# Scores and weights of two of four batch pairs: each half of 64 queries gets a key band of its own

## The chip, the cores and the metric

The kernel runs on one core of one Trainium2 chip. The metric is the device time of one execution in microseconds; the time before is the median of three timed runs. All counts below are of one execution.

## The reference

Eight heads of causal attention with a window of 128 keys and a distance bias, then a two-layer MLP on the concatenated heads. What matters of it:

```python
window, scale = 128, 1.0 / np.sqrt(D)                    # B, H, S, D = 8, 8, 576, 64
scores = scale * np.matmul(q, k.transpose(0, 1, 3, 2))
rel = pos[:, None] - pos[None, :]
mask = (rel >= 0) & (rel < window)
scores = np.where(mask, scores + slopes * (-abs(rel)), -1e9)
attn = np.exp(scores - scores.max(-1))
x = (attn / (attn.sum(-1) + 1e-9)) @ v                   # -> 4608 tokens x 512
h = x @ w_in                                             # 512 x 2048
out = (h * sigmoid(h)) @ w_out                           # 2048 x 512
```

A query at position t attends to positions t-127 to t. A block of 128 queries therefore needs 255 keys, and a half block of 64 queries needs 191.

## The kernel before

**Blocks and pairs.** Two of the eight batches are laid end to end, so there are four batch pairs ("batches" 0 to 3 in the code) of 1152 rows, each of nine blocks of 128 rows: 36 blocks `i`, of which `i >= 18` belong to batches 2 and 3. A block is worked off in two pairs `p = 2i + q`; a pair is four heads, `u` in 0, 1 and `h` in 0, 1. Pairs 36 to 71 are those of batches 2 and 3. Block 0 of a batch pair has no block ahead of it; blocks 4 and 5 (`SPLIT`, `SPLIT + 1`) hold the seam between the two batches.

**One pair, step by step.** `scores` (L510) multiplies the 128 queries by the two key blocks `i - 1` and `i` into two PSUM tiles `sp`, one for each `h`. From batch 2 on, queries and keys are float16 in two parts, so each product is three matmuls (L517 to L523): 24 a pair, 12 in block 0. `h` 0 lies in rows 0 to 63 of the array and `h` 1 in rows 64 to 127, so two matmuls of 64 rows and 128 columns of weights stand side by side. `other_batch` (L533) writes the mask over keys of the other batch, `row_max` (L542) adds the bias table `tab` and takes the row maximum on VectorE, `exps` (L557) runs the exponential on ScalarE. `p_hi` (L572, ScalarE) and `p_lo` (L578; GpSimd for `u` 0, VectorE for `u` 1) split the weights into two float16 parts in a tile `hr` of 128 x 1024, one for each `u`. `p_transpose` (L588) issues one DMA transpose from SyncE's queue for each `u`, into `hl`. `attend` (L613) multiplies by the values: 24 matmuls of 128 x 128 weights and 64 or 65 columns, 12 in block 0. `normalize`, `x_hi`, `x_lo` and `x_dma` pass the result on to the MLP.

**The MLP around it.** Nine groups `g` of 512 tokens go through `gemm1` (L926; the matmuls are L949, L954 or, in the last two groups, L892 and L921) and `gemm2` (L1149; L1165, later L1068). Their matmuls are the bulk of TensorE's work, and a pair's `scores` and `attend` stand between them.

**What sets the order.** All instructions are recorded in the order of a hand-written plan: the loop steps through `pos`, and at each point first runs what `put(point, fn, ...)` has laid there, then one half of `gemm1` or `gemm2` (12 matmuls of 512 columns for most groups). Pair `p` has its scores at point `n = at(p)` (7 or 8 points after those of the pair ahead), `row_max` at n+1, `p_hi` at n+3 and n+4, `p_lo` and `p_transpose` at n+5, `attend` at n+11 or n+12. Each engine takes its instructions strictly in that order.

**Buffers.** `hr` has two buffers, `hl` four, one for each `u`. The tag `w1_2` is a weight tile that is done with before point 150. The scores' PSUM tiles and those of `attend` share the two banks of tag `a`.

Of the kernel before, what the change touches and what calls it, by code (L numbers as in the profile page):

```python
# [6 lines left out]
F32 = mybir.dt.float32  # L7
# [76 lines left out]
X_SUMS = {(NG - 2, 1): X7, (NG - 1, 0): X8, (NG - 1, 1): X9}  # L84
NB = 2
# [61 lines left out]
def tile_window_attention_then_silu_mlp(ctx, tc, qk, v, w_in, w_out, distance, out):  # L147
# [212 lines left out]
    def rescale_bias(b):  # L360

        ratio = vsc[b][:, 8:9] if b > QK16 else vsc[b][:, 7:8]
        flat = tab.rearrange("p h c -> p (h c)")
        nc.vector.tensor_scalar_mul(flat, flat, ratio)
# [140 lines left out]

    def blocks(p):

        return slice(1 if block_of(p // 2) == 0 else 0, 2)

    def scores(p):  # L510
        i, q = divmod(p, 2)
        tags = ("w", "x") if p == 2 * GT else next_tag("scores")
        sp = [ps_of(tags[h], f"sp{p}_{h}").rearrange("p (u o c) -> p u o c", u=2, o=2) for h in range(2)]
        for u in range(2):
            for o in range(blocks(p).start, 2):
                if i >= QK16 * NBLK:
                    for n, (a, b) in enumerate(((0, 0), (1, 0), (0, 1))):  # L517
                        for h in range(2):
                            rows = slice(h * D, (h + 1) * D)
                            nc.tensor.matmul(  # L520
                                sp[h][:, u, o], q16[i][rows, a, 2 * q + u], k16[i - 1 + o][rows, b, 2 * q + u],
                                start=n == 0, stop=n == 2, skip_group_check=True,
                            )  # L523
                    continue
# [17 lines left out]
    def row_max(p, k):  # L542
# [3 lines left out]
        scale, least, op = (1.0, -3.0e38, ALU.max) if b >= QK16 else (-0.125, 3.0e38, ALU.min)  # L546
        for u, h in [(k, 0), (k, 1)] if p < 2 * GT else [(0, k), (1, k)]:
# [9 lines left out]
    def exps(p, u):  # L557
# [6 lines left out]
        for h in range(2):  # L564
            x = t[:, h, 2 * P - n :]
            nc.scalar.activation(x, x, AF.Exp, bias=mx[:, 2 * u + h : 2 * u + h + 1], scale=scale)  # L566

    def split_of(p, u, what):
        n = 2 - blocks(p).start
        return what[:, : 4 * n * P].rearrange("p (a h c) -> p a h c", a=2, h=2)  # L570

    def p_hi(p, u):  # L572
        t, n = st[p]["t"][u], (2 - blocks(p).start) * P
        st[p]["hr", u] = hr = pool.tile([P, 8 * P], F16, tag="hr", bufs=2, name=f"hr{p}_{u}")
# [3 lines left out]
    def p_lo(p, u):  # L578
        t, n = st[p]["t"][u], (2 - blocks(p).start) * P
        hr = split_of(p, u, st[p]["hr", u])  # L580
        if p >= LOW_POOL:
            minus(nc.vector if LOW_DVE and u == LOW_U else nc.gpsimd, hr[:, 1], t[:, :, 2 * P - n :], hr[:, 0])
            return
# [20 lines left out]
    def p_copy_first(p, u):  # L604
        n = 2 - blocks(p).start
        st[p]["hl"][u] = hl = pool.tile([P, 4, P], F32, tag="hl", bufs=4, name=f"hl{p}_{u}")
# [6 lines left out]
    def attend(p):  # L613
# [3 lines left out]
        for u in range(2):  # L617
# [8 lines left out]
            hl = st[p]["hl"][u][:, : 4 * (2 - o0)].rearrange("p (a h o) r -> p a h o r", a=2, h=2)  # L626
            for h in range(2):
                seq = [
                    (hl[:, part, h, o - o0], vp[:, (i - 1 + o) % VSLOTS, 4 * q + 2 * u + h])
# [216 lines left out]
    def x_part(g, t, part):  # L846
        tag, bufs = ("hl", 4) if g == SEVEN else ("rv", 2)
        xsum[g, t, part] = x = pool.tile([P, 2, NCC, P], F16, tag=tag, bufs=bufs, name=f"xs{g}_{t}_{part}")
# [436 lines left out]
    for p in range(NPAIR):  # L1285
# [22 lines left out]
        if block_of(i) in (SPLIT, SPLIT + 1):  # L1308
# [65 lines left out]
    for (g, t), n in X_SUMS.items():  # L1374
        for k, work in enumerate(X_WORK):
            for fn, *a in work:
                put(n + k, fn, g, t, *a)
    put(STATS + 2 * NF + 6, out_scale)
# [212 lines left out]
```

## Time and profile before

| | before |
|---|---|
| median of 3 timed runs | 899.16 us (898.75 to 899.95) |
| profiled execution | 899.22 us |
| its span, first to last instruction | 897.4 us |
| TensorE matmul busy | 890.4 us, 99% |
| VectorE / ScalarE / GpSimd busy | 640.2 / 599.0 / 425.7 us |
| TensorE's granted clock | 2.4 GHz (1.00) over the span |

The profiled execution lasts 1.8 us longer than its span. The page's time slices show TensorE at nine tenths or more in 39 of 40 slices. Matmuls are pipelined: one of 128 columns lasts 216 ns from its start to its end, while the next may start much earlier. What a stretch of matmuls costs is therefore read from starts, that is from the distance between the first start of one group of matmuls and the first start of the next.

### The profile page before, as it was taken

To read this page: it belongs to the slowest core of one execution; us is meant where nothing else is said; L and a number is where in the kernel's file an instruction comes from. 1 tells how busy PE (TensorE), PEld (TensorE's weight loads), DVE (VectorE), ACT (ScalarE), POOL (GpSimd) and SP (SyncE) were. 2 spreads that over 40 slices of the span, in tenths; PEclk is the share of its full clock that TensorE was granted. 3 is DMA by queue.
4 is the path that set the end of the run, shared out by engine and by line. 5 is a ranking of instruction groups with operands and counts; after the bars stand their busy time and mean duration, and the time that the engine had idled before them with its cause. 6 is when DMAs were issued, how large, how long until landed. Compare 5 with 4: busy or idle time off the path is not lost.

```text
span 897.4 us, 20492 instructions
## 1 busy us (share of the span) xinstructions
PE 890.4 (99%) x7801; PEld 592.9 (66%) x7801; DVE 640.2 (71%) x1636; ACT 599.0 (67%) x1321; POOL 425.7 (47%) x492
## 2 busy tenths in 40 slices
PE   9999999999999999999999999999999999999998
PEld 8877777888855555455555555455555557899997
DVE  6998988678876766656776766575775669775665
ACT  7789986776578855778765656565666654465553
POOL 2356652111111212577686766786777412444441
PEclk9999999999999999999999999999999999999999
DMA  8989924335589743868464336353565444400000
GB/s 304 401 199 248 263 60 130 72 94 96 109 212 211 203 101 109 208 156 233 142 153 119 97 108 149 94 134 98 128 139 116 84 95 130 142 26 9 17 26 24
DMA packets 203090, 122.06 MB, mean 136 GB/s; under 512 B 166768, under 2 KB 168944, under 8 KB 202992
## 3 DMA queue, kind: packets, MB, share of 16 engines
q1 hardware_dynamic: 202560, 120.36, 52.1%
q8 instruction: 61, 1.00, 0.5%
q10 hardware_dynamic: 432, 0.39, 0.1%
q14 instruction: 37, 0.30, 0.1%
HBM read 66.72 MB, written 13.63 MB: 90 GB/s over the span
## 4 chain that ended last, share of the span: by engine, by line
PE 92%; DVE 5%; ACT 2%; issue 1%; DMA 0%; DVEq 0%; POOL 0%; POOLq 0%; ACTq 0%
PE o L1165 31%; PE h L949 27%; PE m L1068 7%; PE av L634 5%; PE h L954 5%; PE sp L527 4%; PE h L892 4%; PE sp L520 3%; PE hb L892 3%; PE av L621 1%; PE h L921 1%; PE pt L602 1%; DVE xf L198 0%; PE warm L218 0%; DVE xf L839 0%
## 5 line engine op out<-in xcount | busy, mean ns | idle before, releaser
L949 PE MATMUL h<-xt,w 128*128 128x512 f16 (+1 forms) x1344 | 269.0, 349 | 0.0
L1165 PE MATMUL o<-w,gb 128*128 128x512 f16 x960 | 224.1, 379 | 0.0
L949 PEld LDWEIGHTS <-w 128*128 128x128 f16 x1344 | 126.5, 98 | 112.8 <-issue 3.3
L988 DVE SCALAR_TENSOR_TENSOR h<-gt,h 128x512 f32<-128x512 f32 x112 | 77.7, 694 | 146.8 <-ACT gt L982 146.3
L1165 PEld LDWEIGHTS <-gb 128*128 128x128 f16 x960 | 90.5, 98 | 103.9
L982 ACT ACTIVATE gt<-h,tsc 128x512 f32<-128x512 f32 x104 | 70.9, 681 | 118.8 <-PE h L949 112.8
L196 POOL TENSOR_TENSOR hr<-t,hr 128x512 f16<-128x512 f32 (+1 forms) x54 | 62.8, 1163 | 98.9 <-ACT hr L576 47.6
L196 POOL TENSOR_TENSOR x<-xs,x 128x256 f16<-128x256 f32 x54 | 38.0, 704 | 138.7 <-ACT x L673 114.4
L551 DVE CUSTOM_DVE_ANT_0 t<-sp,tab 128x256 f32<-128x256 f32 (+1 forms) x288 | 100.0, 401 | 2.3 <-PE sp L527 1.7
L1165 PE MATMUL o<-w,gh 128*128 128x512 f32 x256 | 83.0, 405 | 0.5 <-ACT gh L1019 0.5
L566 ACT ACTIVATE t<-t,mx,vsc 128x256 f32<-128x256 f32 (+1 forms) x144 | 74.9, 578 | 1.2
L576 ACT ACTIVATE hr<-t 128x512 f16<-128x512 f32 (+1 forms) x128 | 73.8, 597 | 1.8 <-DMA hl<-hr 1.8
L1023 ACT ACTIVATE gb<-h 128x512 f16<-128x512 f32 x80 | 47.2, 590 | 27.2 <-DVE h L988 26.6
L566 ACT ACTIVATE t<-t,mx 128x256 f32<-128x256 f32 (+1 forms) x144 | 61.7, 487 | 4.6 <-DVE mx L551 3.9
L1037 DVE SCALAR_TENSOR_TENSOR gb<-h,gb 128x512 f16<-128x512 f32 x80 | 54.7, 683 | 12.6 <-ACT gb L1023 12.3
L634 PEld LDWEIGHTS <-hl 128*128 128x128 f16 x1464 | 51.9, 98 | 14.8 <-issue 3.9
L495 POOL TENSOR_SCALAR v<-rv,vsc 128x512 f16<-128x512 f32 x30 | 22.3, 744 | 72.5 <-DMA rv<-v 54.1
L1000 POOL TENSOR_TENSOR gt<-gt 128x256 f32<-128x256 f32 x27 | 21.8, 807 | 71.1 <-DVE gt L991 71.1
L634 PE MATMUL av<-v,hl 128*128 128x65 f16 (+1 forms) x1464 | 55.0, 193 | 0.1
L1165 PEld LDWEIGHTS o<-w,gh 128*128 128x128 f32 x256 | 45.6, 188 | 10.4 <-issue 0.9
L1165 PE MATMUL o<-w,gl 128*128 128x512 f32 x128 | 50.7, 396 | 0.2
L897 ACT COPY hs<-h 128x128 f32<-128x128 f32 x72 | 19.0, 263 | 41.8 <-PE h L892 38.7
(230 smaller groups left out, 1778.3 us busy)
## 6 DMA issues: line engine op xcount, KB each, us to landing
qs<-qk SPq DMA_DIRECT2D x18, 512.0 KB, 4.6
r<-qk SPq DMA_DIRECT2D x18, 512.0 KB, 4.1
wr<-w_in SPq DMA_DIRECT2D x16, 512.0 KB, 6.9
wr<-w_out SPq DMA_DIRECT2D x16, 512.0 KB, 6.7
rv<-v SPq DMA_DIRECT2D x30, 256.0 KB, 3.1
out<-ot SPq DMA_DIRECT2D x28, 256.0 KB, 2.3
vm<-v SPq DMA_DIRECT2D x27, 256.0 KB, 4.7
q<-qk SPq DMA_DIRECT2D x18, 256.0 KB, 3.7
```

The costliest lines, as they stand in the source:

```text
L196: engine.tensor_sub(out, a, b)
L551: nc.vector.tensor_tensor_reduce(out=st[p]["t"][u][:, h, 2 * P - n :], in0=st[p]["sp"][h][:, u, o].rearrange("p o c -> p (o c)"), in1=tab[ ...
L566: nc.scalar.activation(x, x, AF.Exp, bias=mx[:, 2 * u + h : 2 * u + h + 1], scale=scale)
L576: nc.scalar.activation(split_of(p, u, hr)[:, 0], t[:, :, 2 * P - n :], AF.Copy, scale=scale)
L634: nc.tensor.matmul(av[:, 2 * u + h, : rhs.shape[-1]], lhs, rhs, start=(n == 0), stop=(n == len(seq) - 1), skip_group_check=True,)
L892: nc.tensor.matmul(h[to], w_of(j, w, a, cc), x_of(g, t, x, b, cc), start=w in ("11", "S1") and i == 0, stop=i == len(terms) - 1, skip_grou ...
L949: nc.tensor.matmul(o, w[:, wp, cc], x, start=start and k == 0, stop=stop, skip_group_check=True)
L982: nc.scalar.activation(gt, hps[n], AF.Tanh, scale=scale)
L988: nc.vector.scalar_tensor_tensor(out=h, in0=gt, scalar=1.0, in1=h, op0=ALU.add, op1=ALU.mult)
L1037: nc.vector.scalar_tensor_tensor(out=gl, in0=gt, scalar=cut_of(n), in1=f32(gh) if n // NF < OUT16 else gh, op0=ALU.mult, op1=ALU.subtract)
L1068: nc.tensor.matmul(product(k), a[:, k], sum_part(k, j, part), start=j == 0 and side == 0 and a is gh and part == 0, stop=n == last and a i ...
L1165: nc.tensor.matmul(ops[ti], a[:, t], w, start=(f == 0 and i == 0), stop=(f == NF - 1 and i == len(seq) - 1), skip_group_check=True,)
```

## The change

Only batches 2 and 3 (pairs 36 to 71, `banded`) are touched in what they compute with.

- **Scores.** Queries 0 to 63 of a block (half 0) take the 192 keys from the start of block `i - 1` to the middle of block `i`; queries 64 to 127 (half 1) take the 192 keys from the middle of block `i - 1` to the end of block `i`. Each product has 64 rows, 64 columns of weights and 128 or 64 moving columns, and stands in one of four array tiles of 64 x 64: rows by `h`, columns by half. Four such matmuls in a row go to four different tiles. A pair now has 48 score matmuls (24 of 128 columns, 24 of 64), block 0 has 24.
- **Softmax.** `row_max`, `exps`, `p_hi` and `p_lo` run over 192 columns a head in place of 256 (in block 0, over 192 in place of 128). `tab` is cut to 192 columns a half when batch 2 begins (`rescale_bias`: two instructions of 64 rows in place of one).
- **Mask.** `other_batch` writes the columns that lie outside with fewer or more small writes; in block 0 there are four writes a pair where there were none.
- **Transposes.** Both `u` of a pair are written into one tile `hr0` of 128 x 2112 (tag `w1_2`, one buffer for all pairs), whose gaps are cleared once (`clear_room`, point 150, two GpSimd writes). Two DMA transposes a pair take one half of the rows each: 64 rows x 2048 columns, from column 64 for half 0 and column 0 for half 1, so that cleared gaps fill the keys outside the band. Both are issued at `u` = 1. In block 0 they are as long as elsewhere.
- **Buffers.** `hl` becomes two buffers of double size, for all pairs from pair 0 on; `x_part` and `p_copy_first` follow.

`attend` has the same matmuls as before.

```diff
+WIN = P + HALF
+HR_TAG = "w1_2"
+HR_CLEAR = 150
...
     def rescale_bias(b):
         ratio = vsc[b][:, 8:9] if b > QK16 else vsc[b][:, 7:8]
-        flat = tab.rearrange("p h c -> p (h c)")
-        nc.vector.tensor_scalar_mul(flat, flat, ratio)
+        for s in range(2):
+            off = HALF * s if b == QK16 else 0
+            nc.vector.tensor_scalar_mul(
+                tab[halves[s], :, :WIN], tab[halves[s], :, off : off + WIN], ratio[halves[s]]
+            )
...
+    def scores_banded(p, flat):
+        i, q = divmod(p, 2)
+        sp = [a.rearrange("p (u c) -> p u c", u=2) for a in flat]
+        first, second = ((0, i - 1, slice(0, P), 0), (1, i, slice(0, P), HALF)), (
+            (0, i, slice(0, HALF), P), (1, i - 1, slice(HALF, P), 0)
+        )
+        for u in range(2):
+            for both in (first, second):
+                for n, (a, b) in enumerate(((0, 0), (1, 0), (0, 1))):
+                    for s, k, keys, at4 in both:
+                        if block_of(i) == 0 and k < i:
+                            continue
+                        for h in range(2):
+                            rows = slice(h * D, (h + 1) * D)
+                            nc.tensor.matmul(
+                                sp[h][halves[s], u, at4 : at4 + keys.stop - keys.start],
+                                q16[i][rows, a, 2 * q + u, halves[s]], k16[k][rows, b, 2 * q + u, keys],
+                                start=n == 0, stop=n == 2, skip_group_check=True,
+                            )
...
+    OUTSIDE = {0: ((0, P), (1, HALF)), SPLIT: ((1, P),), SPLIT + 1: ((0, HALF),)}
     def other_batch(p):
+        if banded(p):
+            for h in range(2):
+                for s, n in OUTSIDE[block_of(p // 2)]:
+                    nc.vector.memset(st[p]["sp"][h][halves[s], :, :n], MASKED)
+            return
...
+    def clear_room():
+        room[0] = r = pool.tile([P, HALF + 16 * P], F16, tag=HR_TAG, bufs=1, name="hr0_0")
+        gaps = r[:, : 16 * P].rearrange("p (a c) -> p a c", a=8)
+        nc.gpsimd.memset(gaps[:, :, :HALF], 0.0)
+        nc.gpsimd.memset(r[:, 16 * P :], 0.0)
...
     def p_transpose(p, u):
-        st[p]["hl"][u] = hl = pool.tile([P, 8, P], F16, tag="hl", bufs=4, name=f"hl{p}_{u}")
+        if u == 0:
+            st[p]["both"] = pool.tile([P, 2, 8, P], F16, tag="hl", bufs=2, name=f"hl{p}")
+        both = st[p]["both"]
+        st[p]["hl"][u] = hl = both[:, u]
+        if banded(p):
+            if u == 0:
+                return
+            for s in range(2):
+                off = HALF * (1 - s)
+                nc.sync.dma_start_transpose(
+                    both.rearrange("p u a c -> p (u a) c")[:, :, halves[s]], hr[halves[s], off : off + 16 * P]
+                )
+            return
         nc.sync.dma_start_transpose(hl[:, : 4 * n], hr[:, : 4 * n * P])
```

On TensorE, where the scores of pair 38 follow the last matmul of a `gemm1` half (`h52`), this stands in a row before; `sp38_0` and `sp38_1` are the score tiles of `h` 0 and 1, `packed2` holds queries, and the sizes are those of the output:

```order
L949 MATMUL h52_5143<-xt12_3627,w16_0_2_2323 128x512
L520 LDWEIGHTS packed2_5003
L520 MATMUL sp38_0_5162<-packed0_4749,packed2_5003 128x128
L520 LDWEIGHTS packed2_5003
L520 MATMUL sp38_1_5163<-packed0_4749,packed2_5003 128x128
```

and this after, at the step from the products of 128 columns to those of 64:

```order
L553 LDWEIGHTS packed2_4984
L553 MATMUL sp38_0_5156<-packed0_4717,packed2_4984 64x128
L553 LDWEIGHTS packed2_4984
L553 MATMUL sp38_1_5157<-packed0_4717,packed2_4984 64x128
L553 LDWEIGHTS packed2_4984
L553 MATMUL sp38_0_5156<-packed0_4717,packed2_4984 64x64
L553 LDWEIGHTS packed2_4984
L553 MATMUL sp38_1_5157<-packed0_4717,packed2_4984 64x64
```

Twelve couples of a load and a matmul for each `h` have become 24, each with half as many output rows; the work on either side is the same.

On SyncE, which issues the transposes, around pair 38 before (`rv`, `vm`, `qs` and `r16` are loads):

```order
L487 DMA rv19_5211<-v 128x512
L592 DMA_TRANSPOSE hl38_0_5278<-hr38_0_5235 128x8x128
L592 DMA_TRANSPOSE hl38_1_5281<-hr38_1_5249 128x8x128
L249 DMA vm3_3_5286<-v 128x512
L269 DMA qs3_3_5297<-qk 128x2x512
```

and after:

```order
L493 DMA rv19_5229<-v 128x512
L660 DMA_TRANSPOSE hl38_5294<-hr0_0_4009 128x16x64 x2
L252 DMA vm3_3_5301<-v 128x512
L272 DMA qs3_3_5312<-qk 128x2x512
L780 DMA_TRANSPOSE xt16_4832<-x18_5226 128x8x128
```

Both transposes read the one tile `hr0`, and so both stand behind the later of the two `p_lo`.

On VectorE, in block 0 (pair 36), before the row maxima (`ISA`, written to `t36` and `mx36`) there now stand four writes of the mask; before:

```order
L1037 SCALAR_TENSOR_TENSOR gb48_4907<-h48_4866,gb48_4907 128x512
L551 ISA t36_0_4910,mx36_4899<-sp36_0_4885,tab_67 128x128
L551 ISA mx36_4899 128x1
L551 ISA t36_1_4912,mx36_4899<-sp36_0_4885,tab_67 128x128
L551 ISA mx36_4899 128x1
```

and after:

```order
L1116 SCALAR_TENSOR_TENSOR gb48_4887<-h48_4834,gb48_4887 128x512
L567 MEMSET sp36_0_4853 64x2x128
L567 MEMSET sp36_0_4853 64x2x64
L567 MEMSET sp36_1_4854 64x2x128
L567 MEMSET sp36_1_4854 64x2x64
L585 ISA t36_0_4894,mx36_4879<-sp36_0_4853,tab_67 128x192
```

The maxima of block 0 have become half as wide again, and start four writes later.

## Rows read from the trace of the kernel before

**Rows 1.** The page: busy time by engine, granted clock in 40 slices, chain.

```profile
PE 890.4 (99%) x7801; PEld 592.9 (66%) x7801; DVE 640.2 (71%) x1636; ACT 599.0 (67%) x1321; POOL 425.7 (47%) x492
PEclk9999999999999999999999999999999999999999
PE 92%; DVE 5%; ACT 2%; issue 1%; DMA 0%; DVEq 0%; POOL 0%; POOLq 0%; ACTq 0%
```

**Rows 2.** Who TensorE waited for: us in total, times, longest us.

```profile
PE warm L218 <- POOL ident masks.py:199: 1.3, 1, 1.3
PE h L892 <- DVE gt L991: 0.6, 1, 0.6
PE o L1165 <- ACT gh L1019: 0.5, 1, 0.5
PE vs L350 <- DVE row L347: 0.2, 1, 0.2
```

**Rows 3.** Timeline of TensorE around pair 47: start us, us, line, shapes, count.

```profile
470.81 2.75 PE L949 MATMUL h<-xt,w 128*128 128x512 f16 x12
473.50 0.84 PE L520 MATMUL sp<-packed,packed 64*128 64x128 f16 x24
474.27 2.76 PE L1165 MATMUL o<-w,gb 128*128 128x512 f16 x12
...
479.79 0.89 PE L634 MATMUL av<-v,hl 128*128 128x65 f16 x24
480.52 0.38 PE L1165 MATMUL o<-w,gb 128*128 128x512 f16 x1
```

**Rows 4.** Groups by form, matmuls and weight loads: xcount | busy us, mean ns | idle before.

```profile
L634 PEld LDWEIGHTS <-hl 128*128 128x128 f16 x1464 | 51.9, 98 | 14.8 <-issue 3.9
L621 PE MATMUL av<-vf,hl 128*128 128x65 f32 x112 | 13.3, 272 | 0.0
L520 PE MATMUL sp<-packed,packed 64*128 64x128 f16 x696 | 27.3, 217 | 0.0
L520 PEld LDWEIGHTS <-packed 64*128 64x128 f16 x816 | 22.9, 94 | 15.3 <-issue 14.4 <-DVE hr L198 0.8
L602 PEld LDWEIGHTS pt<-ident,t 128*128 128x128 f32 x56 | 6.2, 141 | 1.4 <-ACT t L566 0.7
```

**Rows 5.** Timeline of TensorE around pair 37, a block 0.

```profile
366.53 0.51 PE L520 MATMUL sp<-packed,packed 64*128 64x128 f16 x12
366.97 0.82 PE L1165 MATMUL o<-w,gb 128*128 128x512 f16 x3
```

**Rows 6.** Line L328: a load of one column; duration ns min/median/max.

```profile
L328 PEld LDWEIGHTS vt<-ident,vcol x6: 79/84/84, 314.8 to 477.0; 128*1 128x1 f32 x6
```

**Rows 7.** Timeline of TensorE in the first 36 us: `attend` with float32 weights.

```profile
29.69 1.23 PE L621 MATMUL av<-vf,hl 128*128 128x65 f32 x10
```

**Rows 8.** Groups by form: GpSimd's `p_lo` and VectorE's small mask write.

```profile
L196 POOL TENSOR_TENSOR hr<-t,hr 128x512 f16<-128x512 f32 x48 | 58.5, 1218 | 87.2 <-issue 42.7 <-ACT hr L576 35.8 <-DVE r L655 3.7
L196 POOL TENSOR_TENSOR hr<-t,hr 128x256 f16<-128x256 f32 x6 | 4.3, 724 | 11.8 <-ACT hr L576 11.8
L540 DVE MEMSET sp<- 128x128 f32 x16 | 2.4, 165 | 0.2
```

**Rows 9.** Timeline of the first 0.1 us of pair 47's scores.

```profile
473.50 0.17 PEld L520 LDWEIGHTS <-packed 64*128 64x128 f16 x6 [0.42 <-issue]
473.50 0.28 PE L520 MATMUL sp<-packed,packed 64*128 64x128 f16 x4
```

**Rows 10.** Timeline around pair 55's transposes (SPq is SyncE's queue).

```profile
571.26 0.67 POOL L196 TENSOR_TENSOR hr<-t,hr 128x256 f16<-128x256 f32 x1
571.96 2.96 SPq L592 DMA_TRANSPOSE hl<-hr  x2
576.53 0.53 PE L634 MATMUL av<-v,hl 128*128 128x65 f16 x12
```

**Rows 11.** Line L592, all 128 transposes: issue to landing.

```profile
DMA to landing us min/median/max: 2.3/2.7/7.6
```

More of the change, by code (lines that the diff above doesn't have):

```diff
@@ L504, in v_lo, with banded @@
         )
+    def banded(p):
+        return p >= 2 * QK16 * NBLK
+    halves = (slice(0, HALF), slice(HALF, P))
     def blocks(p):
@@ L513, in scores @@
         sp = [ps_of(tags[h], f"sp{p}_{h}").rearrange("p (u o c) -> p u o c", u=2, o=2) for h in range(2)]
+        if banded(p):
+            scores_banded(p, [a.rearrange("p u o c -> p (u o c)")[:, : 2 * WIN] for a in sp])
+            return
         for u in range(2):
             for o in range(blocks(p).start, 2):
[L516 to L524, printed above, removed]
                 for h in range(2):
@@ L546, in row_max @@
         scale, least, op = (1.0, -3.0e38, ALU.max) if b >= QK16 else (-0.125, 3.0e38, ALU.min)
+        if banded(p):
+            for u in range(2):
+                if u not in st[p]["t"]:
+                    st[p]["t"][u] = pool.tile([P, 2, WIN], F32, tag="t", bufs=3, name=f"t{p}_{u}")
+                nc.vector.tensor_tensor_reduce(
+                    out=st[p]["t"][u][:, k], in0=st[p]["sp"][k][:, u], in1=tab[:, 4 * q + 2 * u + k, :WIN],
+                    scale=scale, scalar=least, op0=ALU.add, op1=op,
+                    accum_out=st[p]["mx"][:, 2 * u + k : 2 * u + k + 1],
+                )
+            return
         for u, h in [(k, 0), (k, 1)] if p < 2 * GT else [(0, k), (1, k)]:
@@ L564, in exps @@
         for h in range(2):
-            x = t[:, h, 2 * P - n :]
+            x = t[:, h] if banded(p) else t[:, h, 2 * P - n :]
             nc.scalar.activation(x, x, AF.Exp, bias=mx[:, 2 * u + h : 2 * u + h + 1], scale=scale)
+    room = {}
+    def clear_room():
[3 more added lines that the diff above has]
+        nc.gpsimd.memset(r[:, 16 * P :], 0.0)
     def split_of(p, u, what):
+        if banded(p):
+            parts = what[:, HALF:].rearrange("p (u a h c) -> p u a h c", u=2, a=2, h=2)
+            return parts[:, u, :, :, :WIN]
         n = 2 - blocks(p).start
@@ L573, in p_hi @@
         t, n = st[p]["t"][u], (2 - blocks(p).start) * P
+        if banded(p):
+            st[p]["hr", u] = hr = room[0]
+            nc.scalar.copy(split_of(p, u, hr)[:, 0], t)
+            return
         st[p]["hr", u] = hr = pool.tile([P, 8 * P], F16, tag="hr", bufs=2, name=f"hr{p}_{u}")
@@ L605, in p_copy_first @@
         n = 2 - blocks(p).start
-        st[p]["hl"][u] = hl = pool.tile([P, 4, P], F32, tag="hl", bufs=4, name=f"hl{p}_{u}")
+        if u == 0:
+            st[p]["both"] = pool.tile([P, 2, 4, P], F32, tag="hl", bufs=2, name=f"hl{p}")
+        st[p]["hl"][u] = hl = st[p]["both"][:, u]
         flat, pt = hl[:, : 2 * n].rearrange("p a c -> p (a c)"), st[p].pop(("pt", u))
@@ L846, in x_part @@
     def x_part(g, t, part):
-        tag, bufs = ("hl", 4) if g == SEVEN else ("rv", 2)
-        xsum[g, t, part] = x = pool.tile([P, 2, NCC, P], F16, tag=tag, bufs=bufs, name=f"xs{g}_{t}_{part}")
+        if g == SEVEN:
+            if part == 0:
+                xsum[g, t] = pool.tile([P, 2, 2, NCC, P], F16, tag="hl", bufs=2, name=f"xs{g}_{t}")
+            xsum[g, t, part] = x = xsum[g, t][:, part]
+        else:
+            xsum[g, t, part] = x = pool.tile([P, 2, NCC, P], F16, tag="rv", bufs=2, name=f"xs{g}_{t}_{part}")
         if part == 0:
@@ L1307, in tile_window_attention_then_silu_mlp @@
         n += p == 4 * GT + 1
-        if block_of(i) in (SPLIT, SPLIT + 1):
+        if block_of(i) in (SPLIT, SPLIT + 1) or banded(p) and block_of(i) == 0:
             put(n + 1, other_batch, p)
@@ L1377, in tile_window_attention_then_silu_mlp @@
                 put(n + k, fn, g, t, *a)
+    put(HR_CLEAR, clear_room)
     put(STATS + 2 * NF + 6, out_scale)
```

13 lines of the change are left out of this document (10 added, 3 removed).

## The prediction, made blind

> **What bounds the kernel now.** I read the page's busy times first. TensorE is busy for 99% of the span, no other engine is above 71%, and the chain that ended last runs over TensorE for 92% of the span [rows 1]. Then I asked who TensorE waited for: four waits over the whole execution, 2.6 us together, none of them for scores or for transposed weights [rows 2]. Its granted clock stands at nine tenths or more in all 40 slices, so the 2.4 GHz level is not in question [rows 1]. So the time is the sum of what TensorE is given to do. A microsecond saved on VectorE, ScalarE or GpSimd (192 columns in place of 256) is worth nothing here by itself, and a microsecond taken off TensorE's own stream is worth a microsecond, as long as nothing newly arrives too late.
>
> **What a score block costs TensorE today.** Pair 47 is a plain one. Its 24 matmuls start at 473.50 and the next line starts at 474.27, so it costs 0.77 us [rows 3]. The last of the 24 starts 0.84 - 0.217 = 0.62 us after the first [rows 3, 4]; two stand side by side (`h` 0 and `h` 1), so this is 11 steps of 56.7 ns, close to 128 columns at 2.4 GHz (53 ns). The rest is a change of array shape: after the last start there pass 0.15 us, of which 0.057 are its own columns, so 0.09 us on leaving; ahead of the first, the last L949 starts at 470.81 + 2.75 - 0.38 = 473.18 and takes one spacing of 0.216 us, so 0.10 us on entering. The new blocks of 64 x 64 tiles also have to change shape twice, so I leave these 0.19 us as they are. A block 0 has 12 matmuls, six steps, and costs 0.44 us [rows 5]. There are 816 loads and as many score matmuls in all [rows 4]: 32 full pairs of 24 and 4 of block 0 of 12.
>
> **What a new block costs.** It has 12 steps again, with four matmuls each, but six of them have 64 columns. The question is how long a step of 64 columns takes. It can't be shorter than its columns: `attend` runs 24 matmuls of 64 or 65 columns in 0.73 us, 30 ns each [rows 3], with a load of weights behind every one. It may be longer if the load of the next weights takes longer than the columns. What a load of 64 columns of float16 costs is not in this trace, so I bound it by three loads that are. A load of one column lasts 84 ns, which is the fixed part [rows 6]. Full loads of 128 float16 columns last 98 ns, 14 more, or 0.11 ns a column [rows 4]. The loads of the float32 transposes last 141, 57 more, or 0.45 ns a column [rows 4]. Where `attend` has float32 weights, its matmuls of 65 columns come every (1.23 - 0.272) / 9 = 106 ns instead of every 30, so there the load sets the step, at 106 / 128 = 0.83 ns a column [rows 4, 7]. Sixty-four columns then cost 7, 29 or 53 ns. I take the middle, 29 ns: float16 has half the bytes of the float32 load that goes at 0.83, and 0.45 is about the pace at which moving columns enter (56.7 / 128 = 0.44) [rows 3]. With 2 ns for the hand-over, a step of 64 columns takes 31 ns and one of 128 stays at 56.7.
>
> A full pair then costs 6 x 56.7 + 6 x 31 = 526 ns of steps against 12 x 56.7 = 680: 154 ns less. Over 32 pairs this is **-4.9 us**. At the cheap end (30 ns) it is -5.1; at the dear end (55 ns, 53 and 2) a pair costs 670 and the gain is 0.3 us.
>
> **Block 0.** Its six steps of 56.7 ns (340 ns) become six of 128 columns and six of 64. The 128s belong to half 1 and the 64s to half 0, so they use different tiles, and a later matmul need not wait for the other tile's columns to end, only for its own tile: about 366 ns, +26. If they do not overlap it is 526, +186. Four pairs: +0.1 to +0.7 us, and I take **+0.2**. The four mask writes (at most 0.165 us each by the nearest row, which is wider) are VectorE's [rows 8]; TensorE has seven or eight points of 12 matmuls (2.76 us for 12 of 512 columns [rows 3]) until it needs these banks again.
>
> **Issuing.** Four starts in a step in place of two. In the first 0.1 us of pair 47 six loads and four matmuls start [rows 9], so ten starts in 100 ns at least are possible; a block of 96 instructions in 0.53 us needs 5.5 ns each. I put **+0.3 us** here (32 x 0.01: the last of four tiles starts a little after the first), and keep the hard case as a rival.
>
> **What leaves TensorE's neighbours alone.** The softmax steps get a quarter shorter in 32 pairs: GpSimd's `p_lo` lasts 1.22 us for 512 columns and 0.72 for 256 [rows 8], so about 0.97 for 384. Both transposes now wait for both `p_lo`. Before, the first was issued behind GpSimd's alone; SyncE needs 1.2 to 1.5 us for one (2.96 for two [rows 10]), so the last landing moves later by 1.4 us at most, and by nothing where GpSimd's `p_lo` is the late one. Behind the waiting transposes on SyncE's queue there stand only loads for later blocks (`vm`, `qs`, `rv`, `r16`, and the `xt` transposes of the MLP's input), which are due many points later. The bytes of the two transposes are what they were, so I leave their median landing at 2.7 us [rows 11]. One place is tight. In pair 55, a block 0, `p_lo` ends at 571.93, the second transpose is issued about 1.5 us after 571.96 and lands 2.3 later (the least of rows 11, which a half-length one has), at about 575.8; `attend` starts at 576.53 [rows 10]. Block 0 now gets a `p_lo` 0.25 us longer and full-length transposes, 0.4 longer (2.7 against 2.3): about 0.1 us of slack is left. Pair 56 right behind it needs both halves at once now. For these two I put **+0.3 us** (0 to 1.5). The single `hr0` makes the next pair's `p_hi` wait for this pair's landing; ScalarE is busy 67% and is not waited for, so nothing. `clear_room` and `rescale_bias` run once or twice, on engines with slack: nothing.
>
> **Sum.** -4.9 + 0.2 + 0.3 + 0.3 = -4.1 us. The profiled execution lasts 899.22 us (span 897.4 and 1.8 around it), 0.06 over the median of the runs; so 899.2 - 4.1 = **895.1 us**, within 893.9 to 897.4 for this case: the cheap end of every term (-5.1 + 0.1) with 0.3 for the trace's own spread, and a gain of only 1.8 us, should issuing and waits take 2.3 us more.
>
> **Rivals.**
>
> *The load sets the step (no change).* If 64 columns load at 0.83 ns each, both kinds of step take 55 to 57 ns: -0.3 us over the full pairs; block 0 goes from 340 to about 460, +0.5; with issuing and waits 0.6: 900.0 us. Should the two halves' loads instead go one after the other at 0.45 ns, a step takes 60 ns: 32 x 40 = +1.3, +0.5 and +0.6: 901.6. The row for it is the float32 `attend`, where exactly this happens [rows 7]; against it, no float16 load of the trace is that slow [rows 4]. The Trainium skill has a rule that speaks for this rival: TensorEngine Tiling (Array Packing), section Restrictions and Gotchas, says that column tiling excludes the fast weight load, and TensorE: Matmul & The Clock Gate, section LDWEIGHTS, gives the load as its columns divided by 1.2 in ns, 53 for 64 columns; by that estimate the time would be this rival's. The trace agrees with the figure for float32 (106 for 128 columns) and not for full float16 loads (14 over the fixed part) [rows 4, 6, 7]. Chance 0.27.
>
> *The loads don't hide (slower).* Now two tiles share the same 64 rows. If a load into one tile has to wait until the neighbour's columns have passed, a step costs columns and load: 6 x (57 + 29) + 6 x (30 + 29) = 870 ns against 680, +190. Over 32 pairs +6.1, block 0 +0.6, and 0.6 as above: 906.5 us. It decides as soon as the mean step exceeds 56.7 ns. Against it: in full tiles the load does hide, since 30 ns a matmul leaves no room beside 27 ns of columns [rows 3]. That page of the Trainium skill, TensorE: Matmul & The Clock Gate, section Part 3: Packing small matmuls, says that a load overlaps matmuls in flight only in other row groups; by it this rival would win. The 30 ns contradict it for full tiles [rows 3]; for column tiles no row shows it. Chance 0.10.
>
> *TensorE's instructions can't come that fast (slower).* The trace's densest runs are 48 instructions in 0.68 us (scores) and 0.73 (`attend`), 14 to 15 ns each [rows 3], but there the columns set the pace. If 14 ns were the sequencer's own limit, a block takes 96 x 14 = 1.34 us, +0.66 over 32 pairs and +0.33 over four: +22 us, 922. Chance 0.05.
>
> *Transposes of 64 rows land later.* If the 64-row form takes 1.5 us more, pair 55, whose slack was 0.7 us, waits 0.8 [rows 10]; with 0.15 on the mean of 36 pairs, an estimate for want of a row for each, that is -4.1 + 5.4: 900.5. For it: no such form is in the trace. Against it: the same bytes. Chance 0.05.
>
> **How the numbers follow.** The forecast has 0.53, the load 0.27, the hidden loads 0.10, issuing 0.05 and the transposes 0.05. The bound between faster, same and slower is 0.2%, 1.8 us, about what a measurement of this kernel can tell from no change: 897.4 and 901.0. Faster: the forecast, 0.53. Same: the load rival, most of it, and half of the transposes: 0.27. Slower: 0.20. The range goes from 893.9 to 903: it leaves out the hidden-loads and issuing rivals and a little at the lower end.
>
> **What would show it.** The new score line's matmuls in a timeline: first start to the next line's start about 0.61 us (0.77 before) in a full pair, and 0.47 (0.44 before) in block 0; steps of 57 and 31 ns. Its loads: a duration near 84 + 29 = 113 ns; near 137 and a block of 0.75 to 0.8 us means the load rival, 0.95 and more means loads that don't hide. TensorE's waits must stay as they are: a line `av` waiting for a DMA on `hl`, at pairs 55 and 56 first, would be the transposes. If the block shrinks to 0.61 us and the time does not, my claim that TensorE's stream alone sets the end is wrong.

## The result: 1.3% slower

The changed kernel takes 910.63 us (median of four runs, 908.67 to 912.05) beside 899.07 for the kernel before: 1.0126 times as long, interval 1.0102 to 1.0149. The profiled execution took 911.7 us with a span of 909.9, 12.5 more than before. The forecast was 895.1 and its range ended at 903.0.

The page of the changed kernel (busy time and instructions, granted clock, queues with packets, MB and share of 16 engines, chain):

```profile
PE 890.5 (98%) x8617; PEld 590.4 (65%) x8617; DVE 640.7 (70%) x1654; ACT 589.3 (65%) x1321; POOL 416.7 (46%) x494
PEclk9999999999999999999999999999999999999999
q1 hardware_dynamic: 206656, 121.41, 57.0%
q8 instruction: 68, 1.11, 0.5%
PE 82%; DVE 6%; ACT 3%; DMA 3%; issue 2%; POOL 2%; SPq 1%; DVEq 0%; POOLq 0%; ACTq 0%
```

TensorE's share of the chain fell from 92% to 82% [rows 1], and what grew are DMA, GpSimd, VectorE, ScalarE, SyncE's queue and "issue": TensorE now waits. Whom it waits for (us in total, times, longest), beside [rows 2]:

```profile
PE av L709 <- issue: 9.5, 10, 2.5
PE warm L221 <- POOL ident masks.py:199: 1.3, 1, 1.3
PE h L971 <- DVE gt L1070: 1.3, 1, 1.3
PE m L1147 <- DVE ot L1263: 0.9, 2, 0.5
...
PE av L709 <- DMA hl<-hr: 0.4, 1, 0.4
```

L709 is `attend`, L971 and L1147 belong to the MLP. "issue" means that the view found no releaser; in these ten pairs the first `attend` matmul starts 0.09 us after the later of the pair's two transposes has landed, so the releaser is the transpose.

To see all of it I summed TensorE's time from each matmul's start to the next one's, by what stands there. The score blocks have the ways in and out with them. "Waits" are what a distance has over the columns' own time (at 2.4 GHz) where that is above 40 ns; the last column holds the rest (columns, short hand-overs, the float32 stages). Each row sums to the span, in us:

| kernel | score blocks | waits of `attend` | waits of the MLP | rest | span |
|---|---|---|---|---|---|
| before | 30.2 | 0.3 | 0.8 | 866.3 | 897.4 |
| after | 26.1 | 12.7 | 4.4 | 866.8 | 909.9 |
| transposes_alone | 30.2 | 9.2 | 0.8 | 866.9 | 907.0 |
| joint_issue | 30.1 | 1.2 | 0.8 | 867.3 | 899.4 |
| two_rooms | 26.0 | 12.3 | 2.6 | 867.0 | 907.8 |
| attend_later | 35.5 | 3.3 | 5.2 | 867.0 | 911.1 |
| old_transposes | 26.0 | 2.3 | 2.2 | 865.9 | 896.5 |
| scores_alone | 26.1 | 0.7 | 6.3 | 868.9 | 901.9 |
| wide_first | 27.6 | 0.3 | 2.8 | 866.9 | 897.5 |
| wide_first_room | 27.6 | 0.3 | 1.8 | 867.7 | 897.3 |
| before_room | 30.1 | 0.3 | 0.1 | 867.1 | 897.6 |
| old_transposes_room | 26.0 | 1.9 | 0.1 | 866.7 | 894.8 |

So the score blocks gave 4.1 us, and `attend` lost 12.4 and the MLP 3.7. In attend_later the score blocks have their own waits in the first column, 9.5 us.

The page's tenths hide one thing: the clock was not as before throughout. Behind the longest wait, that of pair 38, the changed kernel's profiled execution has this (TensorE's timeline, then a stretch with the busy time of each engine; the third number from the end is the granted clock):

```profile
391.71 1.46 PE L1028 MATMUL h<-xt,w 128*128 128x512 f16 x6
395.63 1.04 PE L709 MATMUL av<-v,hl 128*128 128x65 f16 x24 [2.46 <-issue]
396.48 2.75 PE L1028 MATMUL h<-xt,w 128*128 128x512 f16 x6
...
396.20:399.60 3.40, 3.40 (x19) 1.48 (x16) 0.82 (x3) 2.79 (x7) 0.71 (x1) 0.50 1.17 264
```

TensorE stood still for 2.5 us and worked for 0.6 us; then its clock was at 1.2 GHz for 3.4 us, in which it worked without a pause, and six matmuls of 512 columns lasted 2.75 us instead of 1.46 (starts 427 ns apart instead of 216). That is 1.6 of the 3.7 us of the MLP; the other 2.1 are longer waits for VectorE, from 763 to 785 us. The loss doesn't hang on it: the mean clocks of the four executions were 0.997, 1.000, 1.000 and 0.996, their times 911.7, 909.6, 912.1 and 908.7 us.

**The score block.** TensorE around pair 47 of the changed kernel (start us, us, line, count):

```profile
476.42 2.75 PE L1028 MATMUL h<-xt,w 128*128 128x512 f16 x12
479.10 0.72 PE L553 MATMUL sp<-packed,packed 64*64 64x128 f16 x48
479.75 2.76 PE L1244 MATMUL o<-w,gb 128*128 128x512 f16 x12
```

From the first start to the next line it is 0.65 us, in all 32 full pairs, against 0.77 before [rows 3]. The loads, and GpSimd's `p_lo`, by form (xcount | busy us, mean ns | idle before):

```profile
L553 PEld LDWEIGHTS <-packed 64*64 64x64 f16 x1632 | 20.8, 108 | 15.3 <-issue 14.8 <-DVE hr L201 0.4
L199 POOL TENSOR_TENSOR hr<-t,hr 128x384 f16<-128x384 f32 x36 | 36.0, 1000 | 24.2 <-ACT hr L631 24.1
```

**The transposes.** Line L660 between 360 and 755 us; SyncE's time for one (ns, min/median/max), then issue to landing, to be read against [rows 11]:

```profile
L660 SPq DMA_TRANSPOSE hl<-hr x72: 1242/1577/3298, 366.5 to 753.2; - x72
...
DMA to landing us min/median/max: 3.5/4.3/5.9
```

The median is 3.8 us for the first of a pair and 4.4 for the second, against 2.7 and 2.8 before. A full pair still moves 256-byte packets, 1024 a transpose. By the packet records a packet now takes longer: its mean over a transpose was 17.9 ns before and is 26.1 (medians over the transposes).

**One pair, before and after.** Pair 56 in the kernel before: GpSimd's `p_lo`, SyncE's transposes, TensorE.

```profile
581.18 1.60 POOL L196 TENSOR_TENSOR hr<-t,hr 128x512 f16<-128x512 f32 x1
582.80 2.58 SPq L592 DMA_TRANSPOSE hl<-hr  x2
585.55 1.46 PE L949 MATMUL h<-xt,w 128*128 128x512 f16 x6
586.85 0.89 PE L634 MATMUL av<-v,hl 128*128 128x65 f16 x24
```

The same pair in the changed kernel:

```profile
589.11 1.36 POOL L199 TENSOR_TENSOR hr<-t,hr 128x384 f16<-128x384 f32 x1
590.49 3.19 SPq L660 DMA_TRANSPOSE hl<-hr  x2
593.26 1.46 PE L1028 MATMUL h<-xt,w 128*128 128x512 f16 x6
596.25 0.89 PE L709 MATMUL av<-v,hl 128*128 128x65 f16 x24 [1.53 <-issue]
```

Before, `attend` starts 5.67 us after `p_lo` began, and the last transpose lands at 586.91, 0.30 us ahead of the second half of the matmuls (587.21), which alone read it. After, `p_lo` is 0.24 us shorter, but the second transpose, issued at 591.78, lands at 596.16, 5.67 us after the first was issued; before it was 4.11. Now all 24 matmuls need both transposes, since each holds half of the queries of both `u`. TensorE stands still for 1.5 us. Fourteen pairs wait like this, 12.4 us in all: 38 (2.6), 54 (2.1), 56 (1.7), 60 (1.1), 40 (0.9) and nine shorter ones.

### The profile page after: what moved, and what is told of

Read it like the earlier page. It is cut to its first block, busy times and chain, and to the rows that moved or that the text cites. A ratio compares the mean times of both kernels' runs of the same rounds, so it can differ in the third digit from the quotient of the medians.

```text
span 909.9 us, 22102 instructions
## 1 busy us (share of the span) xinstructions
PE 890.5 (98%) x8617; PEld 590.4 (65%) x8617; DVE 640.7 (70%) x1654; ACT 589.3 (65%) x1321; POOL 416.7 (46%) x494
## 4 chain that ended last, share of the span: by engine, by line
PE 82%; DVE 6%; ACT 3%; DMA 3%; issue 2%; POOL 2%; SPq 1%; DVEq 0%; POOLq 0%; ACTq 0%
PE o L1244 27%; PE h L1028 24%; PE m L1147 7%; PE av L709 4%; PE h L1033 4%; PE sp L532 4%; PE h L971 4%; PE hb L971 3%; PE sp L553 2%; DMA hl<-hr 2%; PE av L695 1%; PE h L1000 1%; PE pt L674 1%; DMA rv<-v 1%; ACT t L610 1%
## 5 line engine op out<-in xcount | busy, mean ns | idle before, releaser
L199 POOL TENSOR_TENSOR hr<-t,hr 128x384 f16<-128x384 f32 (+2 forms) x54 | 56.6, 1048 | 90.1 <-ACT hr L635 30.2
L610 ACT ACTIVATE t<-t,mx,vsc 128x192 f32<-128x192 f32 x144 | 68.9, 536 | 1.2
L709 PEld LDWEIGHTS <-hl 128*128 128x128 f16 x1464 | 50.9, 98 | 28.9 <-issue 20.8
L709 PE MATMUL av<-v,hl 128*128 128x65 f16 (+1 forms) x1464 | 55.1, 194 | 10.9 <-issue 9.5
L595 DVE CUSTOM_DVE_ANT_0 t<-sp,tab 128x256 f32<-128x256 f32 (+1 forms) x144 | 50.1, 402 | 2.4 <-PE sp L532 2.2
L199 POOL TENSOR_TENSOR w<-wm,w 128x512 fp32r<-128x512 f32 x32 | 44.9, 1402 | 2.5
```

The lines of the kernel that those rows point to most:

```text
L199: engine.tensor_sub(out, a, b)
L595: nc.vector.tensor_tensor_reduce(out=st[p]["t"][u][:, h, 2 * P - n :], in0=st[p]["sp"][h][:, u, o].rearrange("p o c -> p (o c)"), in1=tab[ ...
L709: nc.tensor.matmul(av[:, 2 * u + h, : rhs.shape[-1]], lhs, rhs, start=(n == 0), stop=(n == len(seq) - 1), skip_group_check=True,)
```

## Experiments on the transposes

**transposes_alone**: the kernel before with the new form of transposes alone, outside of block 0 (scores, widths and masks as before). Both `u` of a pair stand in one row room, two such rooms are used in turn, and `hl` becomes two double buffers as in the change.

```diff
+        if banded(p):
+            if u == 0:
+                return
+            for s in range(2):
+                rows = slice(s * HALF, (s + 1) * HALF)
+                nc.sync.dma_start_transpose(
+                    both.rearrange("p u a c -> p (u a) c")[:, :, rows], st[p]["room"][rows, :]
+                )
+            return
         nc.sync.dma_start_transpose(hl[:, : 4 * n], hr[:, : 4 * n * P])
```

> The kernel before with only the transposes changed in batches 2 and 3, outside of block 0: both u in one tile of 128 x 2048, two DMA transposes of 64 rows x 2048 columns behind both p_lo; two such tiles in turn, hl in two double buffers; scores and softmax as before. Theory 1: transposes land 3.8 and 4.3 us after issue, attend waits, 908 to 916 us. Rival 2 (single hr0): two tiles in turn, so little change, 899 to 901. Rival 3: nothing shorter in TensorE's stream, 899.

Measured: 908.87 us, 1.0098 (1.0083 to 1.0113), as theory 1 had it. `attend` waits 9.2 us. The landing of the new transposes, and the largest of TensorE's waits:

```profile
DMA to landing us min/median/max: 3.6/4.1/5.4
...
PE av L656 <- issue: 5.9, 7, 1.7
```

The transposes by themselves make most of the loss; this kernel has two rooms, so one room is not needed for it.

**joint_issue**: the kernel before, with its old transposes handed to SyncE together, behind both low parts. First in line is the `u` whose low part ended later in the trace of before.

```diff
     def p_transpose(p, u):
+        if p >= 2 * QK16 * NBLK and u == 0:
+            return
+        if p >= 2 * QK16 * NBLK:
+            for k in (0, 1) if p in (40, 47, 51, 54, 55, 56, 59, 60, 63, 64, 65, 67, 68) else (1, 0):
+                one_transpose(p, k)
+            return
+        one_transpose(p, u)
```

> The kernel before with the old transposes (128 rows by 1024 columns, one a u) of batches 2 and 3, but both handed to SP together, behind both low parts, the later one first in line where it is the later by the trace of before. It has the changed kernel's waiting for both low parts without its form of transposes. The last landing moves later by up to one issue, 1.24 us, where the two low parts end close together; in the changed kernel it moves by 1.9 plus 4.3 less 2.7, some 3.5 us. About 11 pairs of before have 1 us of slack or less. Theory 1 (the form is the main term, waiting for both the smaller): 899.5 to 904. Rival (waiting for both low parts is the main term): 906 to 910.

Measured: 900.32 us, 1.0005 (0.9996 to 1.0015), as theory 1 had it. The landing, and the wait of `attend` for transposes:

```profile
DMA to landing us min/median/max: 2.3/2.7/5.3
...
PE av L643 <- DMA hl<-hr: 0.7, 2, 0.5
```

By the table `attend` waits 1.2 us. Waiting for both low parts costs about 1 us (1.0 by the waits, at most 1.4 by the interval), so the form is the main cause.

**packed_dst**: what of the form? This is transposes_alone, with each half's transpose written to 2048 contiguous bytes of a partition in pairs 42 to 53. There the weights don't stand where `attend` reads them; sizes and order are the same.

```diff
+                if 42 <= p < 54:
+                    nc.sync.dma_start_transpose(
+                        both.rearrange("p u a c -> p (u a c)")[:, s * 8 * P : (s + 1) * 8 * P].rearrange("p (a c) -> p a c", c=HALF),
+                        st[p]["room"][rows, :],
+                    )
+                    continue
```

> transposes_alone with, in pairs 42 to 53, a contiguous destination: each transpose of 64 rows by 2048 columns writes 2048 contiguous bytes of a partition instead of 16 runs of 128 bytes. In these pairs the weights stand in the wrong places, so the output isn't the reference's; sizes and order are the same. To be read: landing and time a packet of the transposes of pairs 42 to 53 beside those of the other pairs of the same run. If the 128-byte runs of the destination make the transposes slow, these land in about 2.7 us with 17.6 ns a packet, as before; if the 64 source rows do, they stay at 3.7 to 4.3 us and 24.5 ns.

Measured: 906.23 us in its only execution. The line of pairs 42 to 53, its landing:

```profile
L609 SPq DMA_TRANSPOSE hl<-hr x24: 1252/1536/2332, 430.9 to 552.7; - x24
...
DMA to landing us min/median/max: 3.5/4.2/5.3
```

The other pairs of the same run have 3.7/4.1/5.3, and a packet takes 27.6 ns in the one group and 27.7 in the other (counted as above). Runs of 128 bytes in the destination are not what makes it slow. What is left is the form of 64 rows by 2048 columns; whether the rows or the columns do it, and why a packet takes longer, stays open.

**two_rooms**: the changed kernel with a row room for even pairs and one for odd ones.

```diff
+        for k, tag in enumerate((HR_TAG, "w1_3")):
+            room[k] = r = pool.tile([P, HALF + 16 * P], F16, tag=tag, bufs=1, name=f"hr{k}_0")
...
-            st[p]["hr", u] = hr = room[0]
+            st[p]["hr", u] = hr = room[p % 2]
```

> The changed kernel with two rooms for the weights' rows instead of one, used in turn by pair, so that ScalarE's writes for a pair never wait for the transposes of the pair before. Theory 1 (the loss is the transposes' form and their landing, not the room): 909 to 911. Rival (the single room makes ScalarE wait, and with it the whole chain): 897 to 901.

Measured: 911.41 us, 1.0130 (1.0116 to 1.0144), `attend` waits 12.3 us. The single room costs nothing that these runs can tell, as the prediction had it.

**attend_later**: the changed kernel, with `attend` one point later, as a remedy.

```diff
-            a = n + (... else ATTEND + (...))
+            a = n + (... else ATTEND + (p >= 4 * GT + 2 and banded(p)) + (...))
```

> The changed kernel with attend of pairs 36 to 71 one point of the plan later (some 2.6 us). Theory 1: the waits for hl, some 12 us, all but vanish and the shorter score blocks remain, 895 to 898 us. Rival 2: a wait for the hr0 tile sits ahead of p_hi and is also covered by a later attend, 895 to 898. Rival 3: 895 to 898 too. If TensorE's stream has become longer in another way, or the two banks of tag a are now late, it stays above 905.

Measured: 912.48 us, 1.0135 (1.0119 to 1.0150): the three theories were wrong, and the last case, above 905, came true. TensorE's waits:

```profile
PE sp L553 <- DVE xs L738: 6.3, 10, 1.8
...
PE hb L971 <- DMA wy<-away: 1.2, 1, 1.2
PE av L709 <- issue: 1.1, 1, 1.1
```

The waits of `attend` fell from 12.7 to 3.3 us, but now score blocks wait ten times, put down to VectorE's multiplication behind `attend`: 6.3 us in the view, which counts from a matmul's modelled end, and 9.5 in the table, which counts from its columns. The new wait takes the place of the old one.

**old_transposes**: the changed kernel with the old transposes, one a `u`. The shift by 64 columns of the second half is left out, so the weights of half 1 stand in wrong places.

```diff
-            if u == 0:
-                return
-            for s in range(2):
-                off = HALF * (1 - s)
-                nc.sync.dma_start_transpose(
-                    both.rearrange("p u a c -> p (u a) c")[:, :, halves[s]], hr[halves[s], off : off + 16 * P]
-                )
+            nc.sync.dma_start_transpose(hl, hr[:, HALF + 8 * P * u : HALF + 8 * P * (u + 1)])
```

> The changed kernel with transposes of the old form: one for each u, 128 rows x 1024 columns, behind its own p_lo, from the same single hr0 tile. It leaves out the shift of half 1's columns, so half 1's weights meet the wrong keys; the amount of work is the same. Theory 1: landing back at 2.7 us and p_lo a quarter shorter than before, so attend does not wait, 895 to 897 us. Rival 2: the single hr0 and the double hl are still here, 907 to 911.

Measured: 899.31 us, 0.9994 (0.9985 to 1.0003) of before. The loss is gone, but the 4.1 us of the score blocks are not there either: that had been half of my expectation, and it failed. Beside before, 2.1 us more wait at `attend` (these transposes land in 3.3 us, not 2.7), 1.5 more in the MLP.

## Experiments on the scores

**scores_alone**: the kernel before with four-tile scores; VectorE writes the mask over the columns that are no longer computed. The matmuls are those of the change; the mask:

```diff
...
+            if p >= 2 * QK16 * NBLK:
+                nc.vector.memset(cols[:HALF, :, P + HALF :], MASKED)
+                if block_of(p // 2):
+                    nc.vector.memset(cols[HALF:, :, :HALF], MASKED)
```

> The kernel before with only the score matmuls of batches 2 and 3 in four array tiles; score tiles stay 256 columns wide, the 64 columns outside each band are written by small mask writes on VectorE, and softmax, split and transposes are those of before. Theory 1 (the loss comes from the transposes: the 64-row form lands about 1.5 us later and both now wait for both p_lo, so attend waits): score blocks of 0.65 us in place of 0.77, no new waits of attend beyond about 1 us, 895 to 897 us. Rival 2 (the loss comes from the single hr0 tile and the larger hl buffers, which make the next pair wait for this one): none of these is here, so also 895 to 897. Rival 3 (the way from scores to attend was at its limit already, so any shorter score block is taken back as a wait): 898.5 to 900.

Measured: 904.09 us, 1.0045 (1.0028 to 1.0062): none of the three theories came true. TensorE's waits:

```profile
PE vt L328 <- DVE mx L566: 1.8, 1, 1.8
PE hb L907 <- DMA wy<-away: 1.6, 1, 1.6
...
PE vs L350 <- DVE mx L566: 1.1, 1, 1.1
```

The mask writes stand ahead of VectorE's row maxima, and small matmuls (`vt`, `vs`) wait for these; wide_first, below, has no such writes and neither of the two waits. So this run did not yet tell what the scores alone bring.

**wide_first**: four-tile scores with no new work on VectorE. In the second half of a block the first of the three products still covers all 128 keys, so every column is written.

```diff
...
+                            if n == 0 and keys.stop - keys.start < P:
+                                keys, at4 = slice(0, P), at4 // P * P
```

> The kernel before with its scores of batches 2 and 3 in four array tiles, but without any new work on VectorE: in the second half of a block the product hi by hi still covers all 128 keys (so every column is written), and only the two cross products go down to the 64 keys inside the band. Masks, widths on VectorE and ScalarE, and the transposes are those of before. A pair's columns on TensorE are 1280 instead of 1536 (1152 in the changed kernel), so a score block should take about 0.70 us (0.771 before, 0.649 after). Theory 1 (time saved in the score blocks is kept as long as nothing else in the pair gets longer; scores_alone lost it to its mask writes on VectorE): 32 full pairs by 0.07 us is 2.2 us, less at block 0: 896.5 to 897.5 beside 899.1 for before. Rival (the steps are set by something else, loads or VectorE, and time saved on TensorE's scores always turns into waits): 898.7 to 899.5.

Measured: 900.37 us, 1.0009 (1.0000 to 1.0018). The blocks take 0.70 us as forecast and TensorE's score time falls by 2.6 us, but the time does not fall: the rival was right on that, and the trace shows the place. Its chain around 745 us (start us, us, what):

```profile
744.42 0.69 ACT gt L995
745.10 0.66 ACT ot L1199
745.76 0.02 issue
745.78 4.03 DMA out<-ot
...
749.93 0.75 DVE ot L1197
```

In before the same piece reads:

```profile
747.71 2.02 DMA out<-ot
```

VectorE writes the second output tile of group 6 into the room of the first, and so waits for that one's store. From there the chain runs on VectorE up to 769 us, in both kernels, and TensorE waits for its work at 772.5. Everything in wide_first comes to this place 1.9 us earlier (747.71 - 745.78), but the store lands at 749.80 instead of 749.73. In the records of the packets, all but one of the DMA engines have done their share by 747.44; one starts its eight packets of 2048 bytes only at 748.33, and a packet of 16,384 bytes of the instruction queue lies from 746.67 to 748.34. In before the nearest packets of that queue start at 739.04 and 754.58. That the two share an engine is inferred from the times, since the records don't name it. And this is one execution, the shortest of eleven; how late the store landed in the others is not on record.

**wide_first_room, before_room, old_transposes_room**: wide_first, before and old_transposes (its shift left out again), each with another room for that one tile.

```diff
+        if g == 6 and ti == 1:
+            tag, bufs = "t", 3
```

> wide_first (score blocks 0.70 us, TensorE's score time 2.6 us shorter by its trace, but the same time as before) with one more edit: the second output tile of group 6, which VectorE writes near 750 us, takes a room of the weights' rows (free by then) instead of the room of the first output tile, so VectorE no longer waits for that tile's store to land. In wide_first this wait was 2.65 us (the store landed 4.0 us after its issue; one engine's eight packets started late, behind a 16384-byte instruction packet of 1.67 us), in before 0.64 us (2.0 us to land), and in both VectorE then works without a pause of 0.1 us up to 769 us, and TensorE waits for what it makes at 772.5 us. Theory 1 (the score time saved is lost at that one wait): VectorE's chain starts up to 2.6 us earlier and TensorE's 2.7 us of waits between 750 and 773 go: 896.2 to 897.8 beside 899.4 for before. Rival (VectorE's stage there is bound by something else, or the gain is lost in other places too): 898.8 to 899.8.

> The kernel before with only the other room for the second output tile of group 6, as in wide_first_room. VectorE's wait there is 0.64 us in before and TensorE's at 772.5 us 0.75 us. Theory 1: at most 0.6 us of gain, 898.7 to 899.4 beside 899.4. Rival (the room alone is the gain of wide_first_room): 896.5 to 898.

> old_transposes (the changed kernel with 128-row transposes; half 1's shift is left out, so the output isn't the reference's) with the other room for the second output tile of group 6. Its trace had 2.2 us of TensorE waits from 749 to 772 us beside 0.75 in before, and the store there landed in 3.5 us. Theory 1 (the score term of 4.1 us is there, and was lost mainly at that store): 896 to 898 beside 899.4, with 2.1 us of waits for transposed weights left. Rival: 899 to 900, as without the room.

Measured: wide_first_room 897.67 us, 0.9975 (0.9964 to 0.9986); before_room 899.10, 0.9992 (0.9983 to 1.0001); old_transposes_room 896.52, 0.9962 (0.9948 to 0.9976). All three as theory 1 had it: the room by itself brings nothing that can be told from no change, and with it the score time that TensorE saves shows up, 2.0 of 2.6 us and 3.2 of 4.1. **wide_first_room beats both kernels.** In its profiled execution, its longest, the tile no longer waits for a store:

```profile
L1199 DVE TENSOR_SCALAR ot<-o,gsc x2: 746/746/746, 747.7 to 748.7; 128x512 f32<-128x512 f32 x2
```

and 1.5 us are lost at another load instead. Again an instruction packet (from 773.36, 2.03 us) lies over it, and the load issued at 771.97 took 5.1 us where the same load of before took 3.1; that the packet is the reason is not shown.

```profile
PE hb L905 <- DMA wy<-away: 1.5, 1, 1.5
```

**grown_room**: the changed kernel's transposes up to 360 us, in pairs that the change leaves alone, land in 3.2 us, not 2.8. Its row room is 256 bytes a partition longer than the weights' room that it takes the place of; is that why?

```diff
-            weights[key] = pool.tile([P, 2, DM], F32R, tag=key, bufs=1, name=key)
+            more = 64 if key == "w1_2" else 0
+            flat = pool.tile([P, 2 * DM + more], F32R, tag=key, bufs=1, name=key)
+            weights[key] = flat[:, : 2 * DM].rearrange("p (a m) -> p a m", a=2)
```

> The kernel before with one tile, the weights' room w1_2, made 256 bytes a partition longer (4352 in place of 4096), as the changed kernel makes it for its row room; nothing uses the added bytes. In the changed kernel the transposes of the pairs that the change doesn't touch (8 to 35, up to 360 us) landed in 3.2 us in the median, in before and in transposes_alone in 2.7, and in two_rooms, where two rooms grew by 256 bytes each, in 2.8. Theory (the tiles that lie behind the grown one are moved by 256 bytes, half of 512, and transposes into or out of tiles so placed take longer): all transposes land in about 3.2 us, attend has fewer than 1.5 us of waits for them, and the time is 899 to 902. Rival (the difference comes from other traffic or from the room's own contents): 2.7 us to land, 899 to 900.

Measured: 900.01 us, 1.0000 (0.9991 to 1.0010), landing up to 360 us

```profile
DMA to landing us min/median/max: 2.3/2.8/7.7
```

The theory falls. Why those transposes land later in after and old_transposes, and not in two_rooms, stays open; `attend` did not wait for them.

## Why the prediction was wrong, step by step

*TensorE's stream sets the end.* It held as a sum: the score blocks and the waits of the table give 12.0 of the 12.5 us. But "a microsecond taken off TensorE's own stream is worth a microsecond" did not: wide_first took off 2.6 and got nothing, because VectorE's chain, begun by the wait for a store, sets the pace from 750 to 772 us. The condition put beside it, that nothing newly arrives too late, names the kind of thing and not the place. [Rows 2] had a trace of it, the 0.6 us wait of L892 for VectorE, and I read it as small instead of asking how long VectorE's chain ahead of it is. Nor did the clock, which the kernel before had put out of question, stay at 2.4 GHz: behind the wait of pair 38 it stood at 1.2 GHz for 3.4 us.

*The score block: right.* Steps of mostly 56 and of 28 to 32 ns, read from the starts in the trace, against 56.7 and 31 forecast; loads of 108 ns against 113; block 0 0.455 us against 0.47. A full block took 0.65 instead of 0.61, mostly because the first step takes 80 ns. The three score terms (-4.9, +0.2, +0.3) came to -4.1 instead of -4.4 us. The three rivals on loads and issuing fall by the same steps. By the rule of the Trainium skill behind the first of them (TensorE: Matmul & The Clock Gate, section LDWEIGHTS) a load of 64 columns takes 53 ns, an estimate from its formula. This trace does not agree: each tile gets new weights at every step, and steps of 64 columns last 28 to 32 ns. Behind the second stands the statement of the same page of the Trainium skill, section Part 3: Packing small matmuls, that loads overlap matmuls in flight only in other row groups. This trace does not agree with it either: two column tiles share their rows here, and a step of 64 columns takes little more than its columns (27 ns at 2.4 GHz).

*The transposes: the step that failed.* "The bytes of the two transposes are what they were, so I leave their median landing at 2.7 us." It was 3.8 and 4.4, and from the first issue to the last landing of a full pair there passed 5.7 us instead of 4.2 (medians). Bytes and number of packets did stay; the time of a transpose doesn't follow from them alone. No row showed a transpose of 64 rows, so it should have been bounded from both sides, as the load was, with a dear end of its own; instead I gave it one value in the sum and 0.05 among the rivals.

*The slack: the step that made it dear.* "One place is tight", pair 55, with +0.3 us for it and pair 56; these two waited 1.9 us, and twelve others waited as well. I looked at one pair and reasoned from its being a block 0. In the trace of before, the time from the last landing to the first `attend` matmul, which in the changed kernel needs both transposes, was 1 us or less in five of the 36 pairs and 1.5 us or less in sixteen; in pair 56, a full one, there was none. The rival named the right mechanism, and its 1.5 us were near, but it had 0.15 us a pair, 900.5 us; it was 12.4 us, 0.34 a pair, and 3.7 more in the MLP. With 1.5 us later taken against this slack in every pair, the trace of before gives 7.0 us of waits, an estimate, and so already a loss larger than the gain.

*The single room, GpSimd, the masks: right.* two_rooms shows nothing for the room; `p_lo` takes 1.00 us for 384 columns (0.97 forecast).

## What to carry to other kernels

Before a DMA is given a new shape, measure that shape by itself; the bytes being equal says little, and its delay has to be held against the slack of every place that waits for it, not of the one that looks tightest. And when TensorE is 99% busy, look for the stretch in which another engine's chain has no pause: time saved ahead of it is waited away there, and one wait for a room (here a store's) can hide a real gain until the room is changed.

## What the runs showed of the hardware

- Transposing DMAs of 64 rows by 2048 float16 columns landed in 3.8 us (first of two) and 4.4 (second), of 128 rows by 1024 in 2.7 and 2.8, with as many packets of 256 bytes; a contiguous destination made no difference (4.2 beside 4.1).
- Four 64 x 64 tiles of TensorE took steps of mostly 56 ns for 128 columns and of 28 to 32 ns for 64, weights reloaded at every step, with four matmul starts within about 10 ns.
- After a wait of 2.5 us and 0.6 us of `attend`, TensorE's granted clock stood at 1.2 GHz for 3.4 us, in which 512 columns took 427 ns instead of 216.
- A packet of the instruction queue (16,384 bytes, 1.67 us here, 0.9 to 2.0 elsewhere) by the times fell on one DMA engine's share of a store, which then landed 4.0 us after its issue instead of 2.0. More instructions (61 packets of that queue before, 68 after) move where such packets fall.
